# Queries and keys by token tile and DMA transpose in a fused attention and feed-forward kernel, with moves in SBUF issued by GpSimd

## The chip, the core and the metric

The kernel runs on one NeuronCore of a Trainium2 chip. Its engines have each their own instruction queue and work through it in order: TensorE (PE; matmuls, with weight loads shown apart as PEld), VectorE (DVE), ScalarE (ACT), GpSimd (POOL) and SyncE (SP), which here only issues DMAs. They wait for one another through semaphores. The metric is device time in microseconds, lower is better; it is given as the median of several runs. A profile is one further execution, recorded by the hardware.

## The reference

The input x has 2048 tokens of 448 features in bf16. It is normalised over its features (no learned scale), and two branches read the result; their product is added to x.

```
xn = layernorm(x)
# A: 16 heads of 28 features; token i attends to i, i-2, ..., i-14
q, k, v = split(xn @ wqkv)                 # wqkv: 448 x 1344
o[i]    = softmax_w(q[i] . k[i - 2w] * 28**-0.5) weighted sum of v[i - 2w],  w = 0..7
s       = o @ wo                           # wo: 448 x 448
# B: feed-forward, then silu
g       = silu(gelu(xn @ w1 + b1) @ w2 + b2)   # w1: 448 x 1792, w2: 1792 x 448
out     = x + s * g
```

## The kernel before

**Tokens.** The tokens are read with even ones first and odd ones after them (`tok`, L188), so that a stride of two becomes a stride of one: each half is a sequence of 1024, in which a token attends to itself and the seven before it. There are 16 token tiles of 128 (t = 0..15), in 4 chunks of 512 (c = 0..3). A "chunk" below is one of these.

**Stages of a tile or chunk.** `load_x`, `stats` and `rstds` read x and make its mean and deviation. `norm` (L390) writes the normalised tile xn and turns it into xnT, features on partitions: 448 features are three full groups of 128 and a rest of 64, which is written twice so that two half-height matmuls can run side by side in PE. In chunks 0 and 1 PE turns the tile (L405) and DVE or ACT copies it out of PSUM; in chunks 2 and 3 a DMA transpose issued by SP does (L317). `qk` (L447) makes queries or keys for four heads over 256 tokens (chunk 0) or 512 (the rest): the weights are stationary, xnT streams, and one copy (L270 on ACT, L272 on DVE) puts the result in qT or kT, heads padded to 32 rows. `vproj` (L472) makes values by token tile, xnT stationary. `ff1` (L504) and `ff2` (L529) are the two feed-forward products, `final` (L635) the product with wo, the gating, the sum with x and the store.

**Products in batches.** `batch` (L413) takes products of three full matmuls and a 64-row tail each. It does the full ones of the first jobs ("close"), then all tails in pairs on the two halves of PE, then the full ones of the other jobs ("opened"). Every job of a batch holds a PSUM bank, of which there are eight (`p_b`).

**Attention.** `attn` (L570) works on 17 blocks of up to 128 queries against 128 keys. Scores are 16 small matmuls (L580), one for each head, into four banks; ACT takes exp (L586), DVE multiplies a mask (L594), PE multiplies with the values (L602, "PV"), whose extra column of ones gives the softmax's sum; DVE divides (L609, L614) into `os`. A block's keys start at a multiple of 120 tokens, the value tiles at multiples of 128: `values` (L489) therefore moves pieces of two value tiles into a shifted tile `v` by two DMAs in SBUF (30 in all), and the rows of `os` are moved by 31 such DMAs into token tiles `ot`, which a DMA transpose turns into oT for `final`.

**Order.** The kernel plans its order when it is built. Every step is a task with an engine, an estimated cost, the tasks it waits for and a priority; `_Plan.run` (L79) plays them in time, on each engine the one that can start first, and among those that can start within 0.12 us of it the one with the highest priority. What comes out is the fixed order of each engine's instructions. The chunks' stages are chained by `gate` in the order FF1(0), attention 0 and 1, FF1(1), attention 2, FF1(2), attention 3, FF1(3), so that ACT's tables for exp and gelu are changed seldom. `PRIO` (L704) holds the priorities by chunk. All stores and all moves in SBUF, all transposes and nearly all loads are on SP's queue.

Of the kernel before, what the change touches and what calls it, by code (L numbers as in the profile page):

```python
# [11 lines left out]
ACT = mybir.ActivationFunctionType  # L12
# [141 lines left out]
def kernel(  # L154
# [64 lines left out]
    qT = [sb(f"qT{g}", [P, S]) for g in range(G)]  # L219
    v_tok = [sb(f"v_tok{t}", [P, H, 32]) for t in range(9)]  # L220
    v_tok = v_tok[8:] + v_tok[1:8] + v_tok[:8]
    kT = [sb(f"kT{g}", [P, S]) for g in range(G)]
# [80 lines left out]
    def dma(eng, dst, src, kb, prio, deps=()):  # L303
        def fn(_):
            (nc.sync if eng == "SP" else nc.scalar).dma_start(dst, src)  # L305
        a = plan.add(eng, 0.45, fn, [t_on] + list(deps), prio)
        return plan.add("DMA", kb / (300.0 if prio > 93 else 350.0), lambda _: None, [a], prio, tail=1.7)

    def dma_sb(dst, src, deps, take=(), give=()):
        def fn(k):  # L310
            nc.sync.dma_start(dst(k), src())
        a = plan.add("SP", 0.55, fn, deps, 75, take=take)
        return a, plan.add("DMA", 0.3, lambda _: None, [a], 75, give=give, tail=1.5)

    def dma_T(dst, src, deps, give):
        def fn(_):
            nc.sync.dma_start_transpose(out=dst, in_=src())  # L317
        a = plan.add("SP", 1.3, fn, deps, 70)
        return plan.add("DMA", 0.6, lambda _: None, [a], 70, give=(give,), tail=1.5)
# [70 lines left out]
    def norm(t, prio):  # L390
# [7 lines left out]
        if t >= 2 * TPC:  # L398
            t_xT[t] = dma_T(xnT[:, :, t * P:(t + 1) * P], lambda: buf(p_xn, a)[:], [a], (p_xn, a, 0))
            return  # L400
# [46 lines left out]
    def qk(t0, t1, g, which, prio):  # L447
# [12 lines left out]
        def evac(a, own, i):  # L460
            def fn(k):
                copy(k.on, dst[g][:, cs], buf(p_b, own, i)[:, :n])
# [3 lines left out]
        return _Job(n, full, tail, which, [t_xT[t] for t in range(t0, t1)] + t_wqk[:3], evac, (), t_wqk[3:])  # L466

# [21 lines left out]
    def values(b):  # L489
# [5 lines left out]
        a, d1 = dma_sb(lambda k: buf(p_v, k)[:P - r], lambda: v_tok[t][r:], [t_vt[t]], (p_v,))  # L495
        _, d2 = dma_sb(lambda _: buf(p_v, a)[P - r:], lambda: v_tok[t + 1][:r], [a, t_vt[t + 1]])
# [73 lines left out]
    def attn(b, prio, gate, early):  # L570
# [5 lines left out]
        def f1(k):  # L576
            for g in range(G):
                for hl in range(4):
                    r = slice(32 * hl, 32 * hl + 32)
                    nc.tensor.matmul(buf(p_b, k, hl)[:, g * nq:(g + 1) * nq], kT[g][r, k0:k0 + P],  # L580
                                     qT[g][r, q0:q0 + nq], start=True, stop=True)
# [38 lines left out]
        while q < q0 + nq:  # L620
# [4 lines left out]
                          () if ot[t] else (p_ot,), ((p_os, o, 0),) if q + n == q0 + nq else ())  # L625
            ot[t].append((first, d))
            ot_at[t] = ot[t][0][0]
            if row + n == P:
                t_oT[t] = dma_T(oT[:, :, t * P:(t + 1) * P], lambda t=t: buf(p_ot, ot_at[t])[:], [d for _, d in ot[t]],
# [44 lines left out]
    t_b2 = dma("SP", b2[:], B_b2.rearrange("(o d) -> o d", o=1).to_broadcast((P, D)), 112, 81, [t_hold])  # L674
# [121 lines left out]
```

The softmax here doesn't subtract the row's maximum and nothing guards it: scores larger than these inputs give would overflow.

## Time and profile before

| | |
|---|---|
| median of 8 runs | 168.47 us (167.87 to 169.12) |
| the profiled execution: time | 168.6 us |
| its span, first to last instruction | 166.7 us |
| busy: PE, ACT, DVE, POOL | 159.9, 110.2, 105.1, 4.5 us |
| DMA packets, bytes | 26520, 16.06 MB |
| SP queue: transposes of xn, of ot | 8, 16 |
| SP queue: moves v<-v_tok, ot<-os; stores | 30, 31; 16 |

The profile names an instruction by its line in the kernel, its engine and operation, and by what it writes and reads ("bank<-xnT,w": a PSUM bank from xnT and a weight). A line can be that of a helper: L270 and L272 are the copies of ACT and DVE for whoever asked. "PE busy" counts matmuls whose ends are modelled, so that it can hide short waits. The chain of work that ended last is followed back from the last instruction, step by step, to what released each; where a stretch of it lies on one engine, that engine's own work sets the time there. "x6" after a line is the number of instructions merged into one row; the first two numbers of a row are its start and its length in microseconds.

### The profile page before, as it was taken

How to read it: one execution, taken by the hardware profiler on the slowest of the kernel's cores; microseconds unless marked ns; L12 is line 12 of the kernel's file. 1: busy time of each engine (PE TensorE's matmuls, PEld its weight loads, DVE VectorE, ACT ScalarE, POOL GpSimd, SP SyncE). 2: the span in 40 equal slices, each digit the busy share in tenths (PEclk: the TensorE clock that was granted, in tenths of full speed). 3: DMA queues.
4: the chain of work that ended last, by engine and by line, in shares of the span. 5: the costliest groups of instructions: out<-in, count | busy, mean ns of one | idle time of the engine just before them, and what ended most of it. 6: DMA issues, size and time to landing. Idle time of an engine off the chain costs nothing.

```text
span 166.7 us, 3534 instructions
## 1 busy us (share of the span) xinstructions
PE 159.9 (96%) x1328; PEld 76.9 (46%) x1328; DVE 105.1 (63%) x278; ACT 110.2 (66%) x201; POOL 4.5 (3%) x29
## 2 busy tenths in 40 slices
PE   6999999999999999999999999999999999999980
PEld 2355535454554455434556533543466553345530
DVE  4799993097899968420196920694788987005762
ACT  3286479987888975598866798454895468851210
POOL 7300000000000000000000000000000000000000
PEclk9999999999999999999999999999999999999999
DMA  5999993024183333235313332022123244100101
GB/s 159 263 362 258 359 314 87 0 59 97 35 91 72 86 78 87 58 96 103 75 37 71 73 68 51 0 83 83 28 79 80 51 130 105 38 0 0 55 30 55
DMA packets 26520, 16.06 MB, mean 96 GB/s; under 512 B 14536, under 2 KB 25992, under 8 KB 26504
## 3 DMA queue, kind: packets, MB, share of 16 engines
q1 hardware_dynamic: 26072, 15.39, 35.5%
q10 hardware_dynamic: 432, 0.46, 0.9%
q8 instruction: 10, 0.16, 0.4%
q14 instruction: 6, 0.05, 0.1%
HBM read 7.06 MB, written 1.84 MB: 53 GB/s over the span
## 4 chain that ended last, share of the span: by engine, by line
PE 89%; DMA 5%; DVE 2%; SPq 1%; issue 0%; DVEq 0%
PE bank L536 25%; PE bank L510 23%; PE bank L455 13%; PE bank L639 7%; PE bank L477 5%; PE bank L513 5%; PE bank L602 4%; PE bank L580 3%; DMA wraw<-in_A_wqkv_dram 3%; PE bank L458 3%; DMA v<-v_tok 2%; SPq L305 1%; PE bank L480 1%; PE bank L405 1%; DVE sg L644 1%; DVE o L649 0%
## 5 line engine op out<-in xcount | busy, mean ns | idle before, releaser
L536 PE MATMUL bank<-w,h 128*128 128x448 bf16 x224 | 46.2, 352 | 0.0
L586 ACT ACTIVATE E<-bank 128x480 bf16<-128x480 f32 (+1 forms) x68 | 33.3, 578 | 10.9 <-PE bank L580 10.9
L510 PE MATMUL bank<-xnT,w 128*128 128x512 bf16 x168 | 39.2, 380 | 0.0
L517 ACT ACTIVATE h<-bank,b 128x512 bf16<-128x512 f32 x56 | 34.2, 699 | 5.0 <-PE bank L513 5.0
L536 PEld LDWEIGHTS <-h 128*128 128x128 bf16 x224 | 20.6, 97 | 18.1
L510 PEld LDWEIGHTS <-w 128*128 128x128 bf16 x168 | 15.2, 98 | 21.2 <-issue 5.5
L455 PE MATMUL bank<-xnT,wqk 128*128 128x512 bf16 (+1 forms) x120 | 24.7, 337 | 0.0
L594 DVE TENSOR_TENSOR E<-E,m_gen 128x480 bf16<-128x480 bf16 x60 | 22.3, 404 | 2.5 <-ACT E L586 1.6
L558 ACT ACTIVATE t<-y 128x448 f32<-128x448 f32 x16 | 9.3, 582 | 18.2 <-DVE y L552 18.1
L552 DVE TENSOR_TENSOR y<-bank,b 128x448 f32<-128x448 f32 x16 | 9.9, 621 | 13.5 <-PE bank L536 13.5
L644 DVE SCALAR_TENSOR_TENSOR sg<-bank,g 128x448 bf16<-128x448 f32 x16 | 9.9, 622 | 9.8 <-PE bank L639 9.2
L602 PEld LDWEIGHTS <-E 128*128 128x128 bf16 x272 | 11.4, 96 | 7.9 <-DVE E L594 0.8
L455 PEld LDWEIGHTS <-wqk 128*128 128x128 bf16 x120 | 10.4, 97 | 8.9 <-issue 2.1
L639 PE MATMUL bank<-wo,oT 128*128 128x448 bf16 x64 | 14.1, 352 | 0.0
L270 ACT CAST qT<-bank 128x512 bf16<-128x512 f32 (+1 forms) x17 | 8.5, 500 | 7.1 <-PE bank L458 5.7
L614 DVE TENSOR_TENSOR os<-bank,rd 120x448 bf16<-120x448 f32 (+1 forms) x17 | 10.6, 625 | 3.9 <-DMA ot<-os 3.3
L602 PE MATMUL bank<-v,E 128*128 128x29 bf16 x240 | 11.2, 176 | 0.2 <-DMA v<-v_tok 0.2
L477 PE MATMUL bank<-wv,xnT 128*128 128x448 bf16 x48 | 10.8, 354 | 0.0
L365 DVE BATCH_NORM_STATS2 st<-x_sb 128x6 f32<-128x448 bf16 x16 | 9.6, 603 | 1.5 <-DMA x_sb<-in_A_x_dram 1.4
L562 DVE SCALAR_TENSOR_TENSOR g<-t,y 128x448 bf16<-128x448 f32 x16 | 9.9, 620 | 0.9 <-ACT t L558 0.7
L513 PE MATMUL bank<-xnT,w 64*128 64x512 bf16 x56 | 8.6, 380 | 0.0
L639 PEld LDWEIGHTS <-oT 128*128 128x128 bf16 x64 | 5.9, 97 | 5.2
(60 smaller groups left out, 115.1 us busy)
## 6 DMA issues: line engine op xcount, KB each, us to landing
out_dram<-o SPq DMA_DIRECT2D x16, 112.0 KB
w<-in_B_w_dram SPq DMA_DIRECT2D x1, 1568.0 KB
x_sb<-in_A_x_dram SPq DMA_DIRECT2D x3, 448.0 KB
w<-in_B_w_dram SPq DMA_DIRECT2D x1, 1344.0 KB
wraw<-in_A_wqkv_dram SPq DMA_DIRECT2D x1, 448.0 KB
w<-in_B_w_dram SPq DMA_DIRECT2D x2, 224.0 KB
x_sb<-in_A_x_dram SPq DMA_DIRECT2D x3, 112.0 KB
wo<-in_A_wo_dram SPq DMA_DIRECT2D x1, 336.0 KB
```

What stands on the lines that cost most here:

```text
L455: nc.tensor.matmul(ps[:, :n], wqk[:, kt, hs, :], xnT[:, kt, cs], start=start, stop=stop)
L477: nc.tensor.matmul(ps[:, :D], xnT[:, kt, k0:k0 + P], wv[:, kt, :], start=start, stop=stop)
L510: nc.tensor.matmul(ps[:], w1[:, kt, ms], xnT[:, kt, cs], start=start, stop=stop)
L513: nc.tensor.matmul(ps[:], w1[r, 3, ms], xnT[r, 3, cs], start=start, stop=stop)
L517: nc.scalar.activation(buf(p_h, own, i)[:], buf(p_b, own, i)[:], ACT.Gelu_apprx_tanh, bias=b1[:, mt:mt + 1])
L536: nc.tensor.matmul(ps[:, :D], buf(*h_at[(c, mt)])[:, j * P:(j + 1) * P], w2[:, mt, :], start=(mt == 0), stop=(mt == NMT - 1))
L586: nc.scalar.activation(buf(p_E, k)[:, :, :nq], buf(p_b, a, hl)[:, :4 * nq].rearrange("p (g q) -> p g q", g=4), ACT.Exp, scale=SCALE)
L594: nc.vector.tensor_tensor(out=E[:, :, :nq], in0=E[:, :, :nq], in1=m[:, :, :nq], op=ALU.mult)
L602: nc.tensor.matmul(ps[:, h, :DH + 1], buf(p_E, e)[:, g, :], v[:, h, :DH + 1], start=True, stop=True)
L614: nc.vector.tensor_tensor(out=buf(p_os, k)[:nq, :].rearrange("p (h c) -> p h c", h=H), in0=buf(p_b, po)[:nq, :].rearrange("p (h c) -> p h ...
L639: nc.tensor.matmul(ps[:, :D], oT[:, kt, t * P:(t + 1) * P], wo[:, kt, :], start=(kt == 0), stop=(kt == KT - 1))
L644: nc.vector.scalar_tensor_tensor(out=buf(p_sg, k)[:], in0=buf(p_b, a)[:, :D], scalar=0.5, in1=buf(p_g, t_g[t])[:], op0=ALU.mult, op1=ALU.mult)
```

## The change

It has five parts.

1. In chunk 1 the DMA transpose takes the place of PE's for xnT, as in chunks 2 and 3.
2. In chunks 1 to 3 `qk_rows` takes the place of `qk`: queries or keys of one token tile for all 16 heads, with xnT stationary and the raw weights streaming (448 columns). A copy spreads the 16 heads of 28 features to 16 x 32 columns in a buffer, and a DMA transpose turns that into qT or kT, now one tile each of [128, 4, 2048]. The six buffers are the padded weights of `qk`, which chunk 0 alone still uses; a copy waits for chunk 0's products.
3. The moves in SBUF (v and ot) are issued by GpSimd; SP keeps loads, transposes and stores. Transposes and moves get priorities by chunk, and the planner's costs for them, and for the load of b2 (6.5), are altered.
4. The feed-forward product of chunks 0 and 1 is batched as 4 + 4 and 3 + 3 jobs in place of 2 + 2, 2 + 2 and 2 + 4; in chunk 3 the values are in the same batches as queries and keys.
5. The priorities are altered throughout, with some by token tile.

```diff
--- before.py
+++ after.py
@@ -216,10 +216,10 @@
     b1 = sb("b1", [P, NMT], F32)
     b2 = sb("b2", [P, D])
     xnT = sb("xnT", [P, KT, S])
-    qT = [sb(f"qT{g}", [P, S]) for g in range(G)]
+    qT = sb("qT", [P, G, S])
+    kT = sb("kT", [P, G, S])
     v_tok = [sb(f"v_tok{t}", [P, H, 32]) for t in range(9)]
     v_tok = v_tok[8:] + v_tok[1:8] + v_tok[:8]
-    kT = [sb(f"kT{g}", [P, S]) for g in range(G)]
     oT = sb("oT", [P, KT, S])
     ident = sb("ident", [P, P])
     eps_t = sb("eps_t", [P, 1], F32)
@@ -300,23 +300,24 @@
     t_wo = [plan.add("POOL", 0.45, memset("gpsimd", wo[64:, 3, :], 0.0), [t_on], prio=93)]
     t_E = [plan.add("POOL", 0.1, memset("gpsimd", e[:, :, NQ:], 0.0), [t_on], prio=95) for e in p_E.bufs]
 
-    def dma(eng, dst, src, kb, prio, deps=()):
+    def dma(eng, dst, src, kb, prio, deps=(), issue=0.5):
         def fn(_):
             (nc.sync if eng == "SP" else nc.scalar).dma_start(dst, src)
-        a = plan.add(eng, 0.45, fn, [t_on] + list(deps), prio)
+        a = plan.add(eng, issue, fn, [t_on] + list(deps), prio)
         return plan.add("DMA", kb / (300.0 if prio > 93 else 350.0), lambda _: None, [a], prio, tail=1.7)
 
-    def dma_sb(dst, src, deps, take=(), give=()):
+
+    def dma_sb(dst, src, deps, prio, take=(), give=()):
         def fn(k):
-            nc.sync.dma_start(dst(k), src())
-        a = plan.add("SP", 0.55, fn, deps, 75, take=take)
-        return a, plan.add("DMA", 0.3, lambda _: None, [a], 75, give=give, tail=1.5)
-
-    def dma_T(dst, src, deps, give):
+            nc.gpsimd.dma_start(dst(k), src())
+        a = plan.add("POOL", 0.57, fn, deps, prio, take=take)
+        return a, plan.add("DMA", 0.3, lambda _: None, [a], prio, give=give, tail=2.6)
+
+    def dma_T(dst, src, deps, prio, give):
         def fn(_):
             nc.sync.dma_start_transpose(out=dst, in_=src())
-        a = plan.add("SP", 1.3, fn, deps, 70)
-        return plan.add("DMA", 0.6, lambda _: None, [a], 70, give=(give,), tail=1.5)
+        a = plan.add("SP", 1.28, fn, deps, prio)
+        return plan.add("DMA", 0.6, lambda _: None, [a], prio, give=(give,), tail=1.8)
 
     t_x = {}
 
@@ -395,8 +396,8 @@
             nc.vector.tensor_copy(xn[:, D:], xn[:, KF:D])
 
         a = plan.add("DVE", 0.5, f1, [t_rs[t]], prio, take=(p_xn,))
-        if t >= 2 * TPC:
-            t_xT[t] = dma_T(xnT[:, :, t * P:(t + 1) * P], lambda: buf(p_xn, a)[:], [a], (p_xn, a, 0))
+        if t >= TPC:
+            t_xT[t] = dma_T(xnT[:, :, t * P:(t + 1) * P], lambda: buf(p_xn, a)[:], [a], 105 - 10 * (t // TPC), (p_xn, a, 0))
             return
 
         def f2(k):
@@ -459,11 +460,36 @@
 
         def evac(a, own, i):
             def fn(k):
-                copy(k.on, dst[g][:, cs], buf(p_b, own, i)[:, :n])
+                copy(k.on, dst[:, g, cs], buf(p_b, own, i)[:, :n])
             k = plan.add(("ACT", "DVE"), (act(n), dve(n)), fn, [a], prio + 2, give=((p_b, own, i),))
             for t in range(t0, t1):
                 done[(g, t)] = k
         return _Job(n, full, tail, which, [t_xT[t] for t in range(t0, t1)] + t_wqk[:3], evac, (), t_wqk[3:])
+
+
+    p_qk = _Pool([wqk[:, kt, H * w:H * w + H, :] for kt in range(3) for w in range(2)])
+
+    def qk_rows(t, which, prio):
+        cs = slice(t * P, (t + 1) * P)
+        r = slice(64 * which, 64 * which + 64)
+        dst, done = (kT, t_k) if which else (qT, t_q)
+
+        def full(ps, kt, start, stop):
+            nc.tensor.matmul(ps[:, :D], xnT[:, kt, cs], wraw[:, kt, which * D:(which + 1) * D], start=start, stop=stop)
+
+        def tail(ps, start, stop):
+            nc.tensor.matmul(ps[:, :D], xnT[r, 3, cs], wraw3[r, :], start=start, stop=stop)
+
+        def evac(a, own, i):
+            def fn(k):
+                copy(k.on, buf(p_qk, k)[:, :, :DH], buf(p_b, own, i)[:, :D].rearrange("p (h c) -> p h c", h=H))
+            k = plan.add(("ACT", "DVE"), (act(D), dve(D)), fn,
+                         [a] + [d[g, 0] for d in (t_q, t_k) for g in range(G)] + [d[g, 2] for d in (t_q, t_k) for g in range(G)],
+                         prio + 2, take=(p_qk,), give=((p_b, own, i),))
+            m = dma_T(dst[:, :, cs], lambda: buf(p_qk, k).rearrange("p h c -> p (h c)"), [k], 100 - 10 * (t // TPC), (p_qk, k, 0))
+            for g in range(G):
+                done[(g, t)] = m
+        return _Job(D, full, tail, which, [t_xT[t]], evac)
 
     t_v, v_at, h_at = {}, {}, {}
     t_vt = {}
@@ -492,8 +518,8 @@
         if not r:
             t_v[b], v_at[b] = [t_vt[t]], None
             return
-        a, d1 = dma_sb(lambda k: buf(p_v, k)[:P - r], lambda: v_tok[t][r:], [t_vt[t]], (p_v,))
-        _, d2 = dma_sb(lambda _: buf(p_v, a)[P - r:], lambda: v_tok[t + 1][:r], [a, t_vt[t + 1]])
+        a, d1 = dma_sb(lambda k: buf(p_v, k)[:P - r], lambda: v_tok[t][r:], [t_vt[t]], 98 - 10 * (t // TPC), (p_v,))
+        _, d2 = dma_sb(lambda _: buf(p_v, a)[P - r:], lambda: v_tok[t + 1][:r], [a, t_vt[t + 1]], 98 - 10 * (t // TPC))
         t_v[b], v_at[b] = [d1, d2], (p_v, a, 0)
         v_used[t + 8].append(d1)
         v_used[t + 9].append(d2)
@@ -577,8 +603,8 @@
             for g in range(G):
                 for hl in range(4):
                     r = slice(32 * hl, 32 * hl + 32)
-                    nc.tensor.matmul(buf(p_b, k, hl)[:, g * nq:(g + 1) * nq], kT[g][r, k0:k0 + P],
-                                     qT[g][r, q0:q0 + nq], start=True, stop=True)
+                    nc.tensor.matmul(buf(p_b, k, hl)[:, g * nq:(g + 1) * nq], kT[r, g, k0:k0 + P],
+                                     qT[r, g, q0:q0 + nq], start=True, stop=True)
         a = plan.add("PE", 0.15, f1, deps + early, prio, take=(p_b,) * 4, tail=0.15, mode=32)
         pv, exps = [], []
         for hl in range(4):
@@ -622,11 +648,11 @@
             n = min(P - row, q0 + nq - q)
             first, d = dma_sb(lambda k, t=t, row=row, n=n: buf(p_ot, ot_at.get(t, k))[row:row + n, :D],
                           lambda q=q, n=n: buf(p_os, o)[q - q0:q - q0 + n, :], [o] + t_os + [d for _, d in ot[t]],
-                          () if ot[t] else (p_ot,), ((p_os, o, 0),) if q + n == q0 + nq else ())
+                          90 - 10 * (t // TPC), () if ot[t] else (p_ot,), ((p_os, o, 0),) if q + n == q0 + nq else ())
             ot[t].append((first, d))
             ot_at[t] = ot[t][0][0]
             if row + n == P:
-                t_oT[t] = dma_T(oT[:, :, t * P:(t + 1) * P], lambda t=t: buf(p_ot, ot_at[t])[:], [d for _, d in ot[t]],
+                t_oT[t] = dma_T(oT[:, :, t * P:(t + 1) * P], lambda t=t: buf(p_ot, ot_at[t])[:], [d for _, d in ot[t]], 90 - 10 * (t // TPC),
                                 (p_ot, ot_at[t], 0))
             q += n
         return exps
@@ -671,7 +697,7 @@
     load_x(8, 4, 86, "SP", [t_hold])
     load_x(12, 4, 85, "SP", [t_hold])
     t_w2 = [dma("SP", w2[:], B_w2.rearrange("(m p) c -> p m c", p=P), 1568, 82, [t_hold])]
-    t_b2 = dma("SP", b2[:], B_b2.rearrange("(o d) -> o d", o=1).to_broadcast((P, D)), 112, 81, [t_hold])
+    t_b2 = dma("SP", b2[:], B_b2.rearrange("(o d) -> o d", o=1).to_broadcast((P, D)), 112, 81, [t_hold], 6.5)
     t_wo += [dma("SP", wo[:, 0:3, :], ktiles(A_wo[0:KF, :]), 336, 80, [t_hold]),
              dma("SP", wo[:64, 3, :], A_wo[KF:D, :], 56, 79, [t_hold])]
 
@@ -701,27 +727,42 @@
         t_mask.append(plan.add("DVE", 0.3, fn, [t_m, t_st[3]], prio=60))
 
 
-    PRIO = {"project": (77, 71, 71, 36.5),
-            "attn": (922.5, 900, 875, 876),
-            "ff1": (72.5, 91, 75, 75),
-            "ff2": (63, 73, 3, 5),
-            "final": (52.5, 36.5, 49.5, 49.5, 93.5, 82.5, 101.5, 48.5)}
+
+    FF1 = (((4, 4), (3, 3)),
+           ((4, 4), (3, 3)),
+           ((2, 2), (2, 2), (2, 4)),
+           ((2, 2), (2, 2), (2, 4)))
+    JOINED = (False, False, False, True)
+    PRIO = {"project": (68.5, 142, 73, 262),
+            "attn": (125, 101, 102, 78),
+            "ff1": (55, 127.5, 102, 84.5),
+            "ff2": (37.5, 31, 48, 15.5, 84, 57.5, 53, 61, 42.5, 35.5, 98, 30, 177, 60, 102.5, 49.5),
+            "final": (55.5, 126.5, 96.5, 1, 73.5, 72, 79, 50.5, 70, 19.5, 36, 61.5, 97, 140.5, 122.5, 97.5),
+            "values": (85, 45, 78.5, 77.5),
+            "project2": (86, 54, 70.5, 96),
+            "norm": (34.5, 50, 50, 77.5)}
     blocks_of = [[b for b, (q0, nq, _) in enumerate(BLK) if (q0 + nq - 1) // CH == c] for c in range(NCH)]
     gate = [early]
 
     def project(c):
-        p = PRIO["project"][c]
+        p, pv = PRIO["project"][c], PRIO["values"][c]
         for t in range(c * TPC, (c + 1) * TPC):
-            norm(t, 97 - 2 * t if t < TPC else p + 1)
-        vs = [vproj(t, t % 2, p) for t in range(c * TPC, (c + 1) * TPC)]
+            norm(t, 97 - 2 * t if t < TPC else PRIO["norm"][c])
+        vs = [vproj(t, t % 2, pv) for t in range(c * TPC, (c + 1) * TPC)]
         if c == 0:
             for i in range(0, len(vs), 2):
-                batch(vs[i:i + 1], vs[i + 1:i + 2], 96 if i == 0 else p)
-        for t0, t1 in ((0, 2), (2, 4)) if c == 0 else ((c * TPC, (c + 1) * TPC),):
-            for g in (0, 2):
-                batch(*[[qk(t0, t1, h, w, p) for w in range(2)] for h in (g, g + 1)], p)
-        if c:
-            batch(vs[:2], vs[2:], p - 0.1)
+                batch(vs[i:i + 1], vs[i + 1:i + 2], 96 if i == 0 else pv)
+            for t0, t1 in ((0, 2), (2, 4)):
+                for g in (0, 2):
+                    batch(*[[qk(t0, t1, h, w, p) for w in range(2)] for h in (g, g + 1)], p)
+        else:
+            for t, q in ((c * TPC, p), (c * TPC + 2, PRIO["project2"][c])):
+                js = [[qk_rows(u, w, q) for w in range(2)] for u in (t, t + 1)]
+                if JOINED[c]:
+                    js = [js[i] + [vs[t % TPC + i]] for i in range(2)]
+                batch(*js, q)
+            if not JOINED[c]:
+                batch(vs[:2], vs[2:], pv)
         for b in blocks_of[c]:
             values(b)
 
@@ -746,9 +787,10 @@
         else:
             p = PRIO["ff1"][c]
             hs = [ff1(c, mt, mt % 2, p, gate) for mt in range(NMT)]
-            batch(hs[0:2], hs[2:4], p)
-            batch(hs[4:6], hs[6:8], p - 0.01)
-            ff1_last[c] = batch(hs[8:10], hs[10:14], p - 0.02)
+            i = 0
+            for n, m in FF1[c]:
+                ff1_last[c] = batch(hs[i:i + n], hs[i + n:i + n + m], p - 0.01 * i)
+                i += n + m
             gate = [t_h[(c, mt)] for mt in range(NMT)]
             gels = gate[:-1]
             if c == 0:
@@ -756,9 +798,9 @@
                 project(2)
                 project(3)
             for t in range(c * TPC, (c + 1) * TPC):
-                ff2(t, PRIO["ff2"][c])
+                ff2(t, PRIO["ff2"][t])
     for t in range(NT):
-        final(t, PRIO["final"][t // 2])
+        final(t, PRIO["final"][t])
 
     plan.run()
     with tc.manual_schedule():
```

## The prediction

> **What bounds the kernel now.** I read the page's parts 1 and 2 first, then the waits of TensorE, then the chain in order of time, and last the timelines of SP and of the end.
>
> ```profile
> span 166.7 us, 3534 instructions
> PE 159.9 (96%) x1328; PEld 76.9 (46%) x1328; DVE 105.1 (63%) x278; ACT 110.2 (66%) x201; POOL 4.5 (3%) x29
> PE   6999999999999999999999999999999999999980
> ```
>
> TensorE is busy in every slice except the first and the last two; no other engine passes 66%, and GpSimd does nothing after the start. A busy row can hide waits, so the second view is the list of what PE itself waited for, complete:
>
> ```profile
> PE bank L285 <- DVE eps_t L277: 1.3, 1, 1.3
> PE bank L480 <- DVE xnT L272: 0.5, 1, 0.5
> PE bank L602 <- DMA v<-v_tok: 0.2, 1, 0.2
> ```
>
> Past the warm-up matmuls and the first product, one wait of 0.2 us is all. So between 8.7 us (first product that runs without a wait) and 161.8 us (last product) the time is the sum of what PE is given, and an edit is worth what it takes off PE, less any wait that it adds there. The third view, the chain in order of time, gives the price of each kind of PE work:
>
> ```profile
> 26.69 0.89 PE bank L405 x16
> ...
> 31.11 1.29 PE bank L455 x6
> ...
> 38.44 0.54 PE bank L458 x4
> ...
> 40.15 2.05 PE bank L455 x9
> ...
> 52.95 1.24 PE bank L477 x6
> 54.19 0.48 PE bank L480 x4
> ...
> 57.51 3.96 DMA v<-v_tok
> ...
> 78.88 1.32 PE bank L536 x7
> ```
>
> A 512-column matmul costs 1.29/6 = 0.215 us, a 448-column one 1.32/7 = 0.189. Half-row tails run in pairs: four of 512 columns cost 0.54 = 2 x 0.215 + 0.11, four of 448 columns 0.48 = 2 x 0.189 + 0.10. Nine products after a tail cost 2.05 = 9 x 0.215 + 0.11, so a tail group pays about 0.1 on entering and 0.1 on leaving. The 16 PE transposes of the second chunk cost 0.89. The DMA row is the one move that PE met late: 3.96 us from issue to landing, where the trace's landings give about 2.0 for most others.
>
> **What the Trainium skill says.** (1) "TensorE: Matmul & The Clock Gate", Back-to-back issue gap: a warm matmul of N columns takes N/2.4 + 2.5 ns, 216 for 512 and 189 for 448; the chain agrees (215, 189). (2) "DMA: Bandwidth & Descriptors", SWDGE vs HWDGE vs iDMA: a DMA issued by GpSimd has its descriptors made by software, and Specifications puts its first byte at about 1 us against 0.6 from SP; GpSimd issues none here, so this trace does not show it. (3) The same page, Issuing engines are not separate DMA queues: issuing elsewhere saves only the issuing engine's time. The trace shows that time: the SP timeline has a row of 14 moves lasting 11.44 us, 0.82 each. (4) "SBUF — State Buffer", Who interferes with whom: GpSimd cannot write descriptors while VectorE is in a two-port mode, which copies and tensor_scalar may enter. Candidates here are L393 and L395, 6.3 + 2.9 us in the whole run, so this should touch few moves; no run shows it yet.
>
> **The change, part by part.**
>
> Queries and keys of chunks 1 to 3. Each chunk has 8 outputs of 3 full products and a tail, in two batches. Before: 24 x 0.215 + 2 tail groups of 2 pairs. After, the token tile is stationary and 448 columns stream: the same counts at 0.189. Saved per chunk (24 + 4) x 0.026 = 0.73, in three chunks 2.2 us.
>
> PE transposes of chunk 1: 16 go, 0.89 us, with four copies out of PSUM (three on DVE, one on ACT), which are off the bound.
>
> Batches. Chunks 0 and 1 of the first feed-forward product go from three tail groups to two, with seven pairs either way: 2 x 0.2 = 0.4 us. In chunk 3 the values join the query/key batches, three tail groups become two: 0.2 us. The first batch now fills all eight banks at its tail. ACT empties a bank in about 0.6 us (a row of eight, 4.73 us), PE fills one in 0.77, so PE should find a bank: 0, at worst some 0.5 per batch.
>
> Sum on PE: 2.2 + 0.89 + 0.4 + 0.2 = 3.7 us less.
>
> The end. After the last product comes this on DVE, then the store:
>
> ```profile
> 161.76 0.39 DVE o L649
> 162.15 0.54 DVE g L562
> 162.70 0.03 issue
> 162.73 0.02 DVEq L644
> 162.75 0.04 issue
> 162.79 0.64 DVE sg L644
> ```
>
> The last product ends near 161.8, and its sg starts at 162.79 because g of the last token tile stands ahead of it. The new priorities leave final(3) (priority 1) to last, whose g is long done. That can remove 0 to 0.95 us; I take 0.5.
>
> What it adds off PE. Transposes rise from 24 to 52: 4 of x and 24 of q and k. Each holds SP about 1.23 us and lands 2.45 us after it begins in undisturbed cases (rows of 34.45 to 38.45 us, from the landings). SP loses 61 moves at 0.70 (median), 43 us, and gains 28 x 1.23 = 34 us: lighter, and 52 x 1.23 = 64 us of issue fit in 160. DMA engines: the four transposes from 34.4 us took 0.25 x 2.6 + 0.54 x 3 + some 0.1 x 3, about 2.6 us of all sixteen engines, 0.65 each; 28 more are 18 us, over a present load of 37% of the span. GpSimd gets 61 moves. Bounds for one: an SP move's 0.70 issue and 2.0 landing at the low end; I take the page's extra first-byte time (0.4) and as much again for a software issue, some 3 us; at the high end 1.5 us of issue and 5 us to landing. Even then GpSimd's total is 92 us, so only bursts matter: seven or eight v moves per chunk, with ot moves queued behind them.
>
> Where these can reach PE. q and k formerly became usable one evacuation (0.6 us) after the product; now the eighth transpose of a chunk is issued 7 x 1.23 after the first and lands 2.45 later, about 11 us. Chunk 2 has room: its products run near 40 to 52 us and its scores start at 80. Chunk 3 has none where it stands: products 107.6 to 115.7, first scores 116.9. It must move forward by ten microseconds, and can, since its x is transposed by 74.1; its priority of 262 does so. Chunk 1's x is the tight place:
>
> ```profile
> 10.84 2.17 SPq L305 DMA_DIRECT2D w<-in_B_w_dram  x1
> 13.05 7.11 SPq L305 DMA_DIRECT2D b<-in_B_b_dram  x1
> 20.21 1.16 SPq L305 DMA_DIRECT2D wo<-in_A_wo_dram  x2
> ```
>
> The broadcast load of b2 holds SP for 7.11 us behind the 1.5 MB of w2, and everything queued on SP waits until 20.2; w2 lands at 24.9. The four x transposes would be issued from 20.2 and, behind w2, land near 26 to 28. Chunk 1's first product stood at 31.1, now about 30: covered by 2 us. But its priority (142 against 55 for the feed-forward) may bring it to about 24 in the PE order, and then PE stands up to 2.5 us. I take 0.5 here and 0.5 for all other new waits; the 0.2 us wait of L602 I neither remove nor keep.
>
> Sum: -3.7 - 0.5 + 1.0 = -3.2 us on the 166.7 span, so 163.5. Around it lie 1.9 us (168.6 for the profiled execution), giving 165.4; the median of the runs, 168.47, is 0.1 below that execution, so 165.2.
>
> **The rivals.**
> A, above: PE's saving arrives, with up to 2.5 us of new waits: 163.2 to 167.0. 62%.
> B, no new wait and the whole 0.95 at the end: below 163.2. For it, the present order keeps PE waiting 0.2 us only. Against it, 28 more landings that PE depends on. 7%.
> C, the transposes eat most of it: PE stands 2.5 us for chunk 1's x and a microsecond or so at first scores: 167.0 to 168.0. For it, b2's 7.11 us; against it, the two microseconds of cover. 8%. A little more of the same gives no change, 168.0 to 169.0: 5%.
> D, slower: values arrive late through GpSimd. PE takes its work in order, so a PV group (L602) that waits for v holds the feed-forward products behind it. Fifteen blocks use shifted values; the gain of 4.2 us (3.7 + 0.5) is gone at 0.28 us per block. At 0.5 per block, 7.5 us, the time is 168.5 - 4.2 + 7.5 = 171.8. For it: the one PE wait on a DMA is just this one, and a move that landed 2 us late caused it. Against it: the moves no longer stand behind transposes, and in chunk 0 they land by 29 us for use at 42. 18%.
> That the change does nothing is excluded: the columns streamed are fewer.
>
> **How the numbers follow.** 165.2 is A's. 163.2 leaves B's 7% below. D lies mostly between 169 and 173, with about two thirds above 170: ending at 170 leaves 12% above, 19% in all. A's own range is 163.2 to 167.0. Faster is A + B + C = 77%, same (within 0.3%, about what a measurement of this kernel can tell from no change) 5%, slower 18%.
>
> **What would show it.** PE busy falls by about 3 to 4 us; query/key rows read 128x448 for chunks 1 to 3; only chunk 0's transposes stay at L405; chunk 3's query/key products stand well before 105 us. Among PE's waits there should be less than 2.5 us in all after the first product: on xnT<-xn near 24 to 28 us (C), or on v<-v_tok spread over the blocks (D). GpSimd's moves should land about 3 us after issue. The prediction is wrong if PE's waits exceed 4 us, or if moves take 5 us and more.

## The result, and the profile after

| | before | after |
|---|---|---|
| median (lowest to highest) | 168.23 us (167.73 to 169.12), 31 runs | 166.31 us (165.79 to 167.06), 11 runs |
| ratio, 95% interval | | 0.9886 [0.9868, 0.9904] |
| profiled execution: time, span | 168.6, 166.7 us | 166.27, 164.6 us |
| busy PE, ACT, DVE, POOL | 159.9, 110.2, 105.1, 4.5 us | 156.0, 108.4, 102.8, 37.0 us |
| DMA packets, bytes | 26520, 16.06 MB | 39293, 19.74 MB |

The change takes 1.1% off. Here and below a ratio leaves disturbed executions out, so that it need not be the quotient of two medians.

The head of the page of the kernel after, and PE's row in 40 slices:

```profile
span 164.6 us, 3576 instructions
PE 156.0 (95%) x1312; PEld 75.7 (46%) x1312; DVE 102.8 (62%) x275; ACT 108.4 (66%) x200; POOL 37.0 (22%) x90
PE   6999999999979999998999999999999999999970
```

PE's busy time fell by 3.9 us, the span only by 2.1. The row shows where the rest went: a 7 near 46 us and an 8 near 76 us where before had nines. PE's list of waits, complete (total, times, longest, in us), names them:

```profile
PE bank L285 <- DVE eps_t L277: 1.3, 1, 1.3
PE bank L478 <- DMA xnT<-xn: 1.1, 1, 1.1
PE bank L536 <- DVE wqk L272: 0.8, 1, 0.8
PE bank L506 <- DVE xnT L272: 0.5, 1, 0.5
```

The first and last were there before. The two in the middle are new, 1.08 and 0.76 us, together 1.84. To price PE's work apart from them I summed the time from the start of each matmul to the start of the next, by line, from 8.6 us to the last matmul's start. A wait counts with the matmul ahead of it.

| | before | after | |
|---|---|---|---|
| queries and keys of chunks 1 to 3 | 19.40 | 16.97 | -2.43 |
| PE transposes | 1.46 | 0.48 | -0.98 |
| first feed-forward product | 45.11 | 44.22 | -0.89 |
| PV | 8.03 | 7.80 | -0.23 |
| values | 11.11 | 11.32 | +0.22 |
| product with wo | 11.91 | 12.01 | +0.09 |
| second feed-forward product; both new waits are here | 43.09 | 45.16 | +2.07 |
| everything | 152.76 | 150.61 | -2.15 |

Without the 1.84 us, PE's work is 4.0 us shorter; the waits give nearly half of it back. The chain in order of time shows what stood behind each wait, and the end (start, length):

```profile
28.57 1.14 PE bank L478 x6
...
42.53 4.04 DMA xnT<-xn
...
46.61 1.31 PE bank L478 x6
...
70.23 4.81 DMA qT<-wqk
...
75.14 0.64 DVE wqk L272
...
75.81 2.75 PE bank L536 x12
...
158.87 0.64 DVE sg L670
159.53 0.39 DVE o L675
159.92 0.55 DVE g L588
...
160.56 0.64 DVE sg L670
161.22 0.39 DVE o L675
```

Three readings. Six products of 448 columns cost 1.14 us, 0.19 each, as priced. At 46.6 us chunk 3's first product waits for a DMA transpose of x that took 4.04 us from its start on SP to its landing; at 75.8 us FF1(1) waits for a PSUM bank, which a copy empties only once a buffer `wqk` is free, and that buffer is held by a transpose of q that took 4.81 us. And the end is the same as before: sg, o, g, sg, o on DVE.

SP's timeline around the first of the two waits and after it (start, length, what was issued; a merged row counts its gaps):

```profile
41.22 1.22 SPq L318 DMA_TRANSPOSE kT<-wqk  x1
42.53 6.50 SPq L318 DMA_TRANSPOSE xnT<-xn  x5
49.13 1.91 SPq L318 DMA_TRANSPOSE oT<-ot  x1
51.13 3.86 SPq L318 DMA_TRANSPOSE xnT<-xn  x3
```

One transpose starts within 0.1 us or so of the end of the one ahead of it. From 30 to 84.3 us such rows fill 49.9 of 54.3 us and hold 38 of the kernel's 52 transposes. Before, the same stretch was filled for 43.1 us, with 15 transposes and 30 other DMAs. The moves are on GpSimd now (busy us, mean ns of one; idle before):

```profile
L312 POOL DMA_DIRECT2D v<-v_tok x30 | 16.1, 541 | 57.6 <-ACT v_tok L270 29.9
L312 POOL DMA_DIRECT2D ot<-os x31 | 16.5, 537 | 41.4 <-DVE rd L635 17.9
```

0.54 us each, 33 us in all, and no wait of PE names one.

My theory after this: PE's saving is real, and between 30 and 85 us PE now depends on SP's queue, which is nearly full there, so that a late landing reaches PE; SP would be a second bound. The rivals: the two waits have each a small cause of their own (too few `wqk` buffers; x behind q and k in the queue) that can be removed singly; or GpSimd's moves are at fault, because they make the transposes land late: by the numbers above, neither wait would have been there had the two of 4.04 and 4.81 us landed after 2.45, as in quiet.

### The profile page after: what moved, and what is told of

It reads as the page before. It is cut to its first block, busy times and chain, and to the rows that moved or that the text cites. A ratio compares the mean times of both kernels' runs of the same rounds, so it can differ in the third digit from the quotient of the medians.

```text
span 164.6 us, 3576 instructions
## 1 busy us (share of the span) xinstructions
PE 156.0 (95%) x1312; PEld 75.7 (46%) x1312; DVE 102.8 (62%) x275; ACT 108.4 (66%) x200; POOL 37.0 (22%) x90
## 2 busy tenths in 40 slices
DMA packets 39293, 19.74 MB, mean 120 GB/s; under 512 B 30000, under 2 KB 37828, under 8 KB 39276
## 3 DMA queue, kind: packets, MB, share of 16 engines
HBM read 7.06 MB, written 1.84 MB: 54 GB/s over the span
## 4 chain that ended last, share of the span: by engine, by line
PE 84%; DMA 8%; DVE 4%; SPq 1%; issue 0%; ACT 0%; DVEq 0%
PE bank L562 23%; PE bank L536 23%; PE bank L478 7%; PE bank L665 7%; PE bank L503 5%; PE bank L539 4%; PE bank L628 4%; PE bank L456 3%; DMA wraw<-in_A_wqkv_dram 3%; DMA qT<-wqk 3%; PE bank L606 3%; DMA xnT<-xn 2%; PE bank L481 1%; PE bank L506 1%; SPq L305 1%; DVE wqk L272 1%
## 5 line engine op out<-in xcount | busy, mean ns | idle before, releaser
L312 POOL DMA_DIRECT2D v<-v_tok x30 | 16.1, 541 | 57.6 <-ACT v_tok L270 29.9
L312 POOL DMA_DIRECT2D ot<-os x31 | 16.5, 537 | 41.4 <-DVE rd L635 17.9
L478 PE MATMUL bank<-wraw,xnT 128*128 128x448 bf16 x72 | 16.1, 353 | 1.1 <-DMA xnT<-xn 1.1
L270 ACT CAST wqk<-bank 128x448 bf16<-128x448 f32 x16 | 8.4, 536 | 8.3 <-PE bank L481 6.3
L272 DVE CAST wqk<-bank 128x448 bf16<-128x448 f32 x8 | 5.0, 623 | 11.6 <-PE bank L481 6.8
L503 PE MATMUL bank<-wv,xnT 128*128 128x448 bf16 x48 | 11.3, 353 | 0.0
L640 DVE TENSOR_TENSOR os<-bank,rd 120x448 bf16<-120x448 f32 (+1 forms) x17 | 10.6, 624 | 0.6
```

What stands on the lines that cost most here:

```text
L312: nc.gpsimd.dma_start(dst(k), src())
L478: nc.tensor.matmul(ps[:, :D], xnT[:, kt, cs], wraw[:, kt, which * D:(which + 1) * D], start=start, stop=stop)
L503: nc.tensor.matmul(ps[:, :D], xnT[:, kt, k0:k0 + P], wv[:, kt, :], start=start, stop=stop)
L640: nc.vector.tensor_tensor(out=buf(p_os, k)[:nq, :].rearrange("p (h c) -> p h c", h=H), in0=buf(p_b, po)[:nq, :].rearrange("p (h c) -> p h ...
```

## The experiments

**1. The moves back on SP.** The kernel after, its order kept.

```diff
-            nc.gpsimd.dma_start(dst(k), src())
+            nc.sync.dma_start(dst(k), src())
```

> The changed kernel with the 61 moves in SBUF issued by SP again, the planned order of all work kept. Theory: GpSimd's queue is what makes room for the transposes. Between 30 and 84 us SP issues some 40 transposes, 1.24 us each, 50 us of 54; the 32 moves of that stretch, 0.7 us each, add some 22 us, and PE waits for q and k before attention 1 and 2. At least 5 us slower than the changed kernel, 172 to 188 us. Rival: the late landings (4 to 5 us) come from GpSimd's moves running beside the transposes, so that serial issue on SP would be as good or better: 164.5 to 167 us.

Measured: 180.95 us, ratio to before 1.0753 [1.0723, 1.0783]; 14.6 us above the kernel after. PE's waits (the two longest), and the same kernel in stretches (us, PE busy, PEld, DVE, ACT, POOL; PE's clock; DMA share, GB/s):

```profile
PE bank L606 <- ACT wqk L270: 5.6, 1, 5.6
PE bank L562 <- ACT wqk L270: 3.4, 1, 3.4
```

```profile
60.00:80.00 20.00, 14.42 (x150) 6.42 (x148) 10.18 (x24) 9.86 (x21) 0.00 (x0) 0.83 0.43 96
80.00:100.00 20.00, 16.36 (x105) 6.97 (x104) 6.05 (x15) 9.39 (x18) 0.00 (x0) 0.91 0.40 95
```

The two long waits come through copies to `wqk`, whose buffers wait for transposes of q and k that stand between moves on SP: from 30 to 84.3 us SP issued 29 transposes, not 38. PE's waits are 10.6 us longer than after's in all, and the clock near them, 0.83 and 0.91 for 20 us each, has room for the rest. The late landings went with GpSimd's moves (from 41 to 80 us the transposes landed after 2.3 to 3.0 us), and the time grew all the same: when SP gets to a transpose counts for more here than how long the transpose then takes to land. In this order, part 3 makes the room that parts 1 and 2 use.

**2. Only the moves on GpSimd.** The kernel before, the same edit the other way round, its order kept.

> The kernel before with nothing changed but the issuer of the 61 moves, GpSimd in place of SP, the order kept. Theory: before, PE meets one late move (0.3 us), so the issuer alone is worth nothing by itself: 167.7 to 168.6 us, with moves landing about 2.5 us after issue. Rival: moves made by software land so late that PV products wait: above 169 us.

Measured: 168.67 us, 1.0017 [0.9992, 1.0041]. No wait of PE names v. So the moves by GpSimd neither cost nor win time by themselves: before, SP's load was not what PE waited for. They do change the transposes: 10 of the 24 landed more than 3 us after their start, against 4 of 24 before. In the order of the kernel before, no wait of PE came of it.

**3. Only x of chunk 1 by DMA.** The kernel before; PE's transposes of the chunk and their copies go (those lines are left out here).

```diff
+            if TPC <= t < 2 * TPC:
+                nc.sync.dma_start_transpose(out=xnT[:, :, t * P:(t + 1) * P], in_=xn[:])
```

> The kernel before with chunk 1's x turned by DMA transposes, issued where its normalised tile is ready; PE's 16 transposes and their four copies left out, the rest of the order kept. Theory: what leaves PE is gained, 0.9 to 1.0 us: about 167.2 us. Rival: the four transposes stand behind the load of b2 on SP and land after chunk 1's first product wants them: no gain, 168 us or more, with a PE wait on xnT<-xn near 30 us.

Measured: slower, 1.0142 [1.0111, 1.0174], with a median of 172.86 us (170.47 to 174.16); the profiled execution took 172.25, so that its span is 3.8 us longer than before's, more than the ratio says. From PE's waits, SP's timeline, and PE in stretches (us, PE busy, clock, DMA share, GB/s):

```profile
PE bank L461 <- DMA xnT<-xn: 2.4, 1, 2.4
...
PE bank L608 <- DMA v<-v_tok: 0.6, 1, 0.6
```

```profile
20.42 4.67 SPq L311 DMA_DIRECT2D v<-v_tok  x5
25.19 1.30 SPq L397 DMA_TRANSPOSE xnT<-xn  x1
26.55 1.48 SPq L311 DMA_DIRECT2D v<-v_tok  x2
28.13 3.83 SPq L397 DMA_TRANSPOSE xnT<-xn  x3
```

```profile
33.20:35.40 2.20, 2.18 (x10) 0.64 0.04 10
35.40:42.00 6.60, 6.60 (x52) 0.86 0.38 78
```

The transposes are caught between moves of v, the last starts at 30.7 and lands at 33.2 us, and chunk 1's first product, which before started at 31.1, waits:

```profile
28.07 2.76 PE L516 MATMUL bank<-xnT,w 128*128 128x512 bf16 x11
33.22 2.18 PE L461 MATMUL bank<-xnT,wqk 128*128 128x512 bf16 x6 [2.39 <-DMA xnT<-xn]
```

After the gap PE runs slower: 0.36 x 2.2 + 0.14 x 6.6 = 1.7 us. The starts of the same rows (before's stand in experiment 4) show how it adds up: PE is 0.3 us ahead of before at 28 us, 2.3 behind after the wait, and 3.9 behind once the clock is full again, as it is at the end. The 0.9 us of the transposes is not among it: already ahead of the wait, nothing of it was saved. The wait for v (0.6) is made good later.

**4. Parts 1 and 3 together.** Experiment 3 with the moves on GpSimd.

> The kernel before with chunk 1's x by DMA transpose and the moves issued by GpSimd, the order kept. Theory: alone, the transposes lost 4.5 us because they stood behind seven moves on SP and landed at 33.2 us, after which PE also ran on a lowered clock; with the moves off SP they land near 28 us, before PE wants them at 30: the 0.9 to 1.0 us of PE work is gained, 167.4 us, ratio near 0.994. Rival: b2's load holds SP long enough that PE still waits: 168 us or more.

Measured: 169.29 us, 1.0058 [1.0036, 1.0079]. The waits for x are gone; it lands between 27.9 and 29.4 us. Yet nothing is won; it is even 0.6% slower. PE's timeline of this kernel, then of before:

```profile
27.46 0.37 PE L519 MATMUL bank<-xnT,w 64*128 64x512 bf16 x1 [0.21 <-ACT h L523]
28.03 0.37 PE L519 MATMUL bank<-xnT,w 64*128 64x512 bf16 x1 [0.20 <-ACT h L523]
28.34 2.76 PE L516 MATMUL bank<-xnT,w 128*128 128x512 bf16 x11
30.94 1.46 PE L461 MATMUL bank<-xnT,wqk 128*128 128x512 bf16 x6
```

```profile
26.53 1.06 PE L405 MATMUL bank<-ident,xn 128*128 128x128 bf16 x16
27.52 0.90 PE L513 MATMUL bank<-xnT,w 64*128 64x512 bf16 x6
28.35 2.76 PE L510 MATMUL bank<-xnT,w 128*128 128x512 bf16 x12
30.95 1.46 PE L455 MATMUL bank<-xnT,wqk 128*128 128x512 bf16 x6
```

The 16 PE transposes filled time in which PE has to wait anyhow until ACT's gelu empties banks for the next tails. Taken out alone, they leave a gap of the same length, and the next rows start at the same times. I had not foreseen this, nor did the rival. The 0.7 us by which the span is longer come later, with PE's waits of 0.9 us for an exp near 61 us and 0.2 for v near 122. In the kernel after there is no such gap: its six tails at 27 us run in one row of 0.82 us. That the new batches and order close it is my reading of that row; no run tested them without the rest.

**5. Wider products.** The kernel after, with 512 columns streamed for queries and keys, of which 64 are not used: 28 x 3 x 0.026 = 2.2 us more for PE (0.026 is the difference of the two prices, 0.215 and 0.189). Two small copies on GpSimd make the tail's weights; the order is kept. The line of the full products:

```diff
-            nc.tensor.matmul(ps[:, :D], xnT[:, kt, cs], wraw[:, kt, which * D:(which + 1) * D], start=start, stop=stop)
+            nc.tensor.matmul(ps[:, :512], xnT[:, kt, cs], wraw[:, kt, 384 * which:384 * which + 512], start=start, stop=stop)
```

> The changed kernel with 512 columns streamed in place of 448 for queries and keys of chunks 1 to 3 (64 of them unused), the order kept; two small copies on GpSimd make the tail's weights. PE gets 84 pair or single passes of 64 more columns, 2.2 us. Theory: the two waits of PE (1.1 us at 46.6 us on xnT<-xn, 0.8 us at 75.8 us on a buffer that a q transpose holds) are set by the time at which SP gets to its transposes, so they shrink as PE gets later: 0.7 to 1.5 us slower than the changed kernel. Rival: the waits go along with PE, each follows a PE product at a fixed distance: the full 2.2 us slower, 168.5 us.

Measured: 166.67 us, 0.9917 [0.9886, 0.9948]; 0.4 us above the kernel after, and the intervals overlap. Both new waits are gone from PE's list. 2.2 more of work less 1.84 of waits is 0.4: PE's own work ahead of such a wait is nearly free. How much of this is PE's later arrival the profile doesn't tell by itself, for in it the two transposes also landed sooner, 3.2 and 3.6 us after their start in place of 4.0 and 4.8.

**6. More work for SP.** The kernel after, with two idle transposes behind the last one of chunk 1's x (into a part of oT that is written again later; `X7` holds the target of that last one).

```diff
+            if any(dst is d for d in X7):
+                for i in range(2):
+                    nc.sync.dma_start_transpose(out=oT[:, :, (14 + i) * P:(15 + i) * P], in_=w2[:, 0:2, :].rearrange("p m c -> p (m c)")[:, :512])
```

> The changed kernel with two idle transposes more on SP (of w2 into a part of oT that is written again later), right behind the last x transpose of chunk 1; no other engine gets anything. Theory: SP is the second bound between 30 and 85 us, where its issues stand nearly end to end (50.3 of 54.3 us), so 2.6 us more on SP come out as 1.5 to 2.7 us more in the end: 167.8 to 169.0 us, ratio to before 0.998 to 1.005. Rival: the two waits are accidents of single late landings and the queue has room: below 0.7 us more, ratio below 0.993.

Measured: 168.15 us, 0.9974 [0.9951, 0.9998], above the kernel after by 1.8 us (by the ratios, 1.5). The two hold SP from 29.57 us for 2.57. PE's waits:

```profile
PE bank L542 <- DVE wqk L272: 1.3, 1, 1.3
...
PE bank L484 <- DMA xnT<-xn: 1.0, 1, 1.0
...
PE bank L634 <- ACT E L618: 0.7, 1, 0.7
```

These 2.57 us on SP's queue cost 1.5 to 1.8, while 2.2 more on PE cost 0.4. With experiment 1, this shows that in this order the time hangs on SP's queue in that stretch. Whether it would in any order is for 11 and 12.

**7. Eight buffers for q and k.** `wqk3` and `warm` join the six, taken in turn.

```diff
+    p_qk.bufs += [wqk3[:], warm[:].rearrange("p (h c) -> p h c", h=H)]
+    for i, k in enumerate(k for k in plan.order if p_qk in k.slots):
+        k.slots[p_qk] = [i % 8]
```

> The changed kernel with eight buffers in place of six between the query/key copies and their transposes (the padded tail weights and the warm-up tile, both idle by then), the order kept. Theory: PE's wait of 0.8 us at 75.8 us hangs on a buffer that a q transpose frees late, so it goes: about 0.7 us faster than the changed kernel, ratio to before near 0.984. Rival: the feed-forward batch that starts there then waits for the next thing, banks or ACT: no gain, ratio 0.988 to 0.990.

Measured: 165.88 us, 0.9841 [0.9806, 0.9876]. The wait for `wqk` is gone; another came:

```profile
PE bank L665 <- DMA oT<-ot: 1.2, 1, 1.2
PE bank L478 <- DMA xnT<-xn: 0.6, 1, 0.6
```

**8 and 9. Chunk 3's x earlier.** In SP's order its four transposes go ahead of the last three of chunk 1's q and k; in 9 together with 7.

```diff
+    _T = [k for k in plan.order if k.on == "SP" and "dma_T" in k.fn.__qualname__]
+    _x = [k for k in _T if k.prio == 75]
+    _q = sorted((k for k in _T if k.prio == 90), key=lambda k: k.start)[:8]
+    for k in _x[:4]:
+        k.start = _q[5].start - 0.001
+    plan.order.sort(key=lambda t: (t.start, t.seq))
```

> The changed kernel with the four x transposes of chunk 3 issued ahead of the last three q and k transposes of chunk 1 on SP, all else kept. Theory: PE's wait of 1.1 us at 46.6 us on xnT<-xn is one of SP's order and goes, and since nothing needs those q and k before 60 us, about 1.0 us is gained, ratio to before near 0.982. Rival: what is gained at 46.6 us comes back at 75.8 us, where PE waits for a buffer that SP's later transposes free: below 0.3 us gained.

> Both: eight buffers and the x transposes of chunk 3 first. Theory: both waits go, 1.8 us faster than the changed kernel, 164.5 us, ratio to before about 0.977. Rival: a third wait takes their place, on oT<-ot or on the exp of a late score: 165.3 us or more.

Measured: 8 gave 166.79 us, 0.9908 [0.988, 0.9937], no gain; 9 gave 165.78 us, 0.9868 [0.9829, 0.9908]. In 9 the one long wait left is for oT too, 0.9 us. PE's new waits of 8:

```profile
PE bank L665 <- DMA oT<-ot: 1.0, 1, 1.0
PE bank L536 <- DVE wqk L272: 0.8, 1, 0.8
PE bank L628 <- ACT wqk L270: 0.5, 1, 0.5
```

Each time a wait was taken away, a wait for another transpose took its place. Patches to single waits do not help much; the small gain of 7 and 9 can't be told from nothing against the kernel after (the intervals overlap).

**10. Less on DVE at the end.** Experiment 7, with the sum o of token tile 14 on GpSimd.

```diff
-            nc.vector.tensor_tensor(out=buf(p_o, k)[:], in0=x_sb[:, t, :], in1=buf(p_sg, s)[:], op=ALU.add)
+            (nc.gpsimd if t == NT - 2 else nc.vector).tensor_tensor(out=buf(p_o, k)[:], in0=x_sb[:, t, :], in1=buf(p_sg, s)[:], op=ALU.add)
```

> The changed kernel with eight query/key buffers, and the last sum of the second-last token tile on GpSimd in place of DVE, the order kept. Theory: after the last product DVE has sg, o, g, sg, o in a row, 2.7 us; with one o (0.39 us) off it the end comes 0.3 to 0.4 us earlier than in the run with eight buffers alone: ratio to before about 0.982. Rival: GpSimd's sum is so slow that its store is the last to land: no gain, 0.984 or more.

Measured: 168.19 us, 0.9964 [0.9939, 0.9989], some 2.3 us worse than 7 (by the ratios, 2.1); its profiled execution took 169.57, so what follows is read from a longer one than most. Its timeline near the end:

```profile
160.61 1.37 POOL L675 TENSOR_TENSOR o<-x_sb,sg 128x448 bf16<-128x448 bf16 x1 [22.40 <-DVE sg L670]
```

The sum takes 1.37 us on GpSimd against 0.39 on DVE. The last store landed 4.0 us after PE's last matmul had started, as in the kernel after (4.1), so nothing was won. In the records of the end, the other engines then waited for GpSimd for 2.4 us, against 0.04 after, while a drain on GpSimd lasted 6.5 us. Why it took so long is open.

**11 and 12. The order planned with later landings.** The kernel after with eight buffers; the planner is told that a transpose holds SP for 1.32 (12: 1.34) us and that its tail is 2.8 (2.6), not 1.8; and the priorities, now with some for the transposes and stores, are searched anew with these costs. Nothing that the engines compute changes. The costs of 11, without the new priorities and buffers:

```diff
-        a = plan.add("SP", 1.28, fn, deps, prio)
-        return plan.add("DMA", 0.6, lambda _: None, [a], prio, give=(give,), tail=1.8)
+        a = plan.add("SP", 1.32, fn, deps, prio)
+        return plan.add("DMA", 0.6, lambda _: None, [a], prio, give=(give,), tail=2.8)
```

> The changed kernel with eight buffers and another order: the planner is told that a transpose holds SP for 1.32 us and lands 4.8 us after it begins (it believed 3.9), and the priorities are chosen for the shortest planned time under that. Theory: what the change lost to waits was lost because the order left landings too little time; with time left for them PE's waits shrink to a few tenths and 1 to 2 us come back: 164.2 to 165.3 us, ratio 0.975 to 0.982. Rival: the waits come from SP's total of transposes, which no order removes: 165.8 us or more.

> The same with 1.34 us on SP and 4.6 us to landing, another set of priorities. Theory and rival as for the order before: 164.3 to 165.5 us against 165.8 us or more.

Measured: 165.02 us, 0.9772 [0.9719, 0.9824], and 165.04 us, 0.9779 [0.9721, 0.9836]: both beat both kernels, by 1.3 us the kernel after. PE's waits of 12, complete:

```profile
PE bank L298 <- DVE eps_t L290: 1.3, 1, 1.3
PE bank L520 <- DVE xnT L285: 0.4, 1, 0.4
PE bank L679 <- DMA oT<-ot: 0.2, 1, 0.2
PE bank L620 <- DVE wqk L285: 0.2, 1, 0.2
```

The first two stood in before as well; of the 1.84 us, 0.4 remain. So the rival that no order removes these waits falls. Neither the queue nor the landings got lighter: from 30 to 84.3 us SP is filled for 50.5 and 50.2 of 54.3 us (49.9 in the kernel after), with 39 and 38 transposes, and of all 52, 24 and 27 landed more than 3 us after their start (23 in the kernel after). A full queue and late landings, then, cost PE time only through an order that needs their results sooner. The two runs don't separate what did it: later landings in the plan, the two buffers, or merely a better order found by a new search. Against experiment 7 alone (165.88) the gain is 0.85 us, and the intervals overlap a little. Whether the waits would go in the order of the kernel after, too, if GpSimd's moves delayed no transpose, was not tested.

## Why the prediction came out as it did

It said 165.2 us, and that its case A (PE's saving arrives, with some waits) was likeliest; measured are 166.31 us, inside A's own range, 163.2 to 167.0. The case is the right one, but the gain is 1.9 us and not 3.3, and part of the agreement is luck: the range allowed up to 2.5 us of waits, and the waits that filled it were not those foreseen. Point by point:

- **PE as the bound, and the sum of PE's work: right.** 3.7 us were predicted, 4.0 measured: queries and keys 2.2 and 2.43; PE transposes 0.89 and 0.98; batches of the first feed-forward product 0.4 and 0.89. The prices by column from the chain hold for the new form: 0.19 us for 448 columns. The formula that the prediction took from the Trainium skill ("TensorE: Matmul & The Clock Gate", Back-to-back issue gap) gives the same, but the page has it for a single isolated matmul, and puts a stream of matmuls with their weight loads at about 131 ns for 512 columns; the trace's stream takes 215, so the formula fits here and that figure does not. The joined batch's 0.2 did not show: values cost 0.22 more. But the terms don't stand alone: the 0.89 of the transposes was filler in the order before (experiment 4), and taking it out pays only if nothing else leaves the gap.
- **New waits: the term that was mis-sized.** 1.0 us predicted, 1.84 measured, and not where I put them. At chunk 1's x, my tight place and rival C's, nothing waited: b2 held SP for 8.17 us, the four transposes landed between 28.1 and 30.4 us, and the first product came at 28.57. I had no named place for the other 0.5; it became 1.84 us at 46.6 and 75.8.
- **The step behind it that failed: "SP loses 61 moves ... lighter, and 52 x 1.23 = 64 us of issue fit in 160".** Right as an average, and it hid that 38 of the 52 fall in 54 us, where SP is 92% filled (49.9 of 54.3). I asked whether SP had time in the run, not whether it got to each transpose before its result was needed. The filling alone is not the fault, since 11 and 12 are as full and wait less. The other end of it is the buffers: I took "2.45 us in undisturbed cases" for the landing, and did not ask how long a slow landing holds one of the six buffers, and through its copy a PSUM bank.
- **The end: failed.** I took 0.5 us for final(3) going last; measured is nothing. final(3) runs earlier in the planned order despite its priority. And no priority could have put it last to any gain: in both kernels the products of final(14) and final(15) wait alike for the second feed-forward product of tile 15 (`t_f2[min(t + 1, NT - 1)]` in `final`), so that both stand behind it, and g of tile 15 still lies between two sums. Priority 1 says what goes last among the ready ones, and not what is ready last. With the end at 0 and the waits at 1.84, the sum -3.7 - 0.5 + 1.0 is -4.0 + 1.84 = -2.2 on the span, against 2.1 measured.
- **Rival D, values late through GpSimd: not so.** No wait of PE names v. I had bounded a move at 3 us to landing; the median is about 2.8, with 6 to 7 during the loads at 10 to 17 us, when nobody is waiting. What the skill has on VectorE's two-port mode ("SBUF — State Buffer", Who interferes with whom) does not show in the time: experiment 2 is 1.0017 [0.9992, 1.0041]. Whether single moves were held up by it was not looked at. What the moves did delay, the transposes, the prediction had at nothing.
- **"Issuing elsewhere saves only the issuing engine's time"** ("DMA: Bandwidth & Descriptors", Issuing engines are not separate DMA queues; the page calls that time usually small relative to the DMA itself). That time was worth 14.6 us in the order of the kernel after (experiment 1) and nothing in that of the kernel before (experiment 2). And it was not the only thing that changed: in both orders more transposes landed late with the moves on GpSimd (the counts are in the last section).

## What to carry to other kernels

When work moves to a queue, weigh the queue's load in the stretch in which the results are needed, and not over the whole run; and count how long each slow landing holds a buffer, and who waits for that buffer. A full queue is no loss by itself; a result that is needed before the queue delivers it is. In an order fixed beforehand, leave room for landings as late as they come under load; here orders planned so were faster, though the runs don't show that this alone did it. An operation taken off the bound gives its time back only if nothing else was going to be waited for there; undoing one part at a time in a fixed order shows which parts carry each other.

## What was not expected of the hardware

- A [128 x 512] bf16 transpose in SBUF holds SP for 1.22 us and lands 2.3 to 2.45 us after its start, unless something else runs. In the kernel after, 23 of the 52 took over 3 us, many of them 4 to 5. Two things stand beside the late ones. One is a packet of the instruction queue, of 8 or 16 KB; those of 16 KB lasted 0.9 to 1.6 us on one DMA engine. At 34.65 us, for example, the transposes around it landed after 4.75 and 3.99 us, and one held SP for 2.44. The other is GpSimd's moves, and three pairs of kernels differ in nothing but their issuer. With the moves on GpSimd 23 of 52 transposes took over 3 us in the kernel after, 10 of 24 in experiment 2 and 14 of 28 in experiment 4; with them on SP it was 8 of 52 in experiment 1, 4 of 24 in the kernel before and 2 of 28 in experiment 3, and each of these fourteen had an instruction packet during its flight. So moves issued by GpSimd do make transposes land later here. How is open: on GpSimd's queue the moves run beside the transposes, on SP's they stand between them. The packets were not varied. Of the two that PE waited for in the kernel after, the first had no such packet in its flight, the second had one (at 72.7 us).
- A gap of 2.4 us in PE's work was followed by a mean clock of 0.64 for 2.2 us and 0.86 for 6.6 more (experiment 3). Both means come of one stretch at half clock in the trace's record, 3.4 us long, from 33.8 us. The Trainium skill ("TensorE: Matmul & The Clock Gate", What's actually happening) has the clock lowered after at least one idle window of about 3.4 us; a gap of 2.4 us was enough here.
- A sum of 128 x 448 in bf16 takes 1.37 us on GpSimd against 0.39 on DVE, and in the profiled execution with it near the end GpSimd came 2.4 us late to the end of the program (experiment 10).
